# One of three shifted copies made by a pre-filled buffer and an adding DMA, in a two-kind attention stack

## The chip, the cores and the metric

The kernel runs on one core of one Trainium2 chip. The metric is device time in microseconds (us) of one execution; lower is better. The core has TensorE (PE; its weight loads are listed as PEld), VectorE (DVE), ScalarE (ACT), GpSimd (POOL), a queue that mostly issues DMAs (SP), and 16 DMA engines.

## The reference

Four residual blocks follow one another on x of 2048 rows by 512 columns, bf16: A, B, A, B with shared weights.

```python
# A: 32 query heads of 16, one shared key head and one shared value head
q = (x @ wq).reshape(B, S, H, Dh).transpose(0, 2, 1, 3); k = x @ wk; v = x @ wv
scores = einsum("bhqd,bkd->bhqk", q, k) * Dh ** -0.5
p = softmax(scores, axis=-1)
o = einsum("bhqk,bkd->bhqd", p, v)          # then heads joined, @ wo
# B: linear attention, phi(t) = where(t > 0, t + 1, exp(t)) + 1e-6
kv = einsum("bhsd,bhse->bhde", phi(k), v); z = sum over s of phi(k)
o = einsum("bhqd,bhde->bhqe", phi(q), kv) / (phi(q) . z + 1e-6)   # then @ wo
x = x + A(ln(x)); x = x + B(ln(x)); x = x + A(ln(x)); x = x + B(ln(x))
```

## The kernel before

All data stay in the core's own memory from the first load to the last store. The text calls the two A blocks layer 0 and layer 2, and the two B blocks layer 1 and layer 3. Nearly all time goes into the exponentials of A: 32 heads of 2048 by 2048 scores, cut into 4096 blocks (two layers of 2048) of 128 keys (partitions) by 512 columns, the columns being 4 heads' worth of 128 queries. Line 933 makes one block of scores in a PSUM bank, on one of four row groups of TensorE; blocks of different row groups are issued together. The blocks are grouped into segments of 64 (one query tile, one half of the heads, all 16 key tiles and 4 lanes; some segments are split by key tiles at the start of a layer). Then a block takes one of two ways:

- **The ScalarE way.** Two or three blocks at once are exponentiated by one ACTIVATE (line 1109) into a `PT` buffer, and each block is multiplied by the values with one matmul (line 987, weights `V`).
- **The VectorE way.** VectorE adds a constant to the scaled scores, clamps them and converts to int16 (line 1190). Read as bf16, these bits are a coarse power of two. To smooth it, three more copies are made with w*32 added to the bits, w = 1, 2, 3 (line 1232), and the four copies are multiplied by the values with four different weights `VW` (line 987, four matmuls). A **chunk** is up to four such blocks in one `FB` buffer of 128 x 2048 int16; the three shifted copies go to three more `FB` buffers, each with one instruction over the whole chunk.

`FB` buffers come from `fb_pool`: 12 of its own, and others that are lent while their owner is idle (`sacc` 1, `xn` 1, `wq` 1, `wo2` 1, and in layer 2 two in `OBB`). The same line of code can therefore appear in the profile as writing `FB`, `wq`, `xn`, `OBB`, `sacc` or `wo`; the page prints the buffers of `wo2` as `wo`.

Which block goes which way, and the order of instructions on each engine, is fixed when the program is built. The `Planner` runs the whole work as a simulation of events: each `op` has a duration per engine, a priority, a delay `lat` until its result is seen, and dependences; free buffers are handed out by pools; the order in which the simulation starts ops is the order written into each engine's queue, with semaphore waits. On the chip each engine then goes through its queue strictly in that order. An op that takes longer on the chip than in the plan therefore holds up whatever is queued behind the instruction that waits for it. `dve_hit` opens a chunk only while more than `FBO` buffers are free; VectorE is given a block only while its backlog is short (`dve_open`, `dve_split`, `alone`), so a faster VectorE is given more blocks. `dve_close` starts `dve_shifts`, which asks for a buffer for each shifted copy:

```python
for w in range(1, NSH):
    ...
    g_ = yield ("acq", fb_pool, pr)
    ...
    o = op({en: (du, lambda e, w=w, g_=g_: e.tensor_scalar(
        out=fbs[g_][:, 0:n].bitcast(I16), in0=fbs[f_][:, 0:n].bitcast(I16), scalar1=float(w * 128 // NSH), scalar2=None, op0=ALU.add))},
```

`spend` returns a buffer to the pool when the last of its users is done, and `pv_post` puts the blocks on the list from which `pv_try` builds groups of up to four matmuls for the segment that is being summed. Plain loads, stores and DMA transposes (`dmat`, used for 24 transposes `OT<-Osb` and 36 `xnT<-xn`) go through SP. In layers 0 and 2 POOL does one power per row tile (line 789, part of the layer norm, for which VectorE's line 792 waits) and one small product (line 836). `fill` (line 1032) gives TensorE dummy matmuls when it has nothing else to do.

Of the kernel before, what the change touches and what calls it, by code (L numbers as in the profile page):

```python
# [8 lines left out]
I16 = mybir.dt.int16  # L9
ACTF = mybir.ActivationFunctionType  # L10
ALU = mybir.AluOpType
# [4 lines left out]
P = 128  # L16
# [7 lines left out]


class Op:
    __slots__ = ("eng", "opts", "fn", "deps", "prio", "left", "users", "done", "end", "n", "value", "sem", "signal", "isdma", "name", "freed", "begun", "slot", "cols", "mode", "port")


class Pool_:  # L30
# [5 lines left out]
class Planner:  # L36
# [3 lines left out]
    def __init__(self, nc):  # L40
        self.nc = nc
        self.now = 0.0
        self.events = []
        self.seq = 0
        self.ready = {e: [] for e in ENGS}
        self.busy = {e: False for e in ENGS}
        self.until = {e: 0.0 for e in ENGS}
        self.order = {e: [] for e in ENGS}
        self.writer = {}
        self.readers = {}  # L50
        self.flags = {}
# [5 lines left out]
        self.port = 0.0  # L57
        self.calm = False
        self.hungry = []
        self.near = {e: [] for e in ENGS}  # L60
# [12 lines left out]
    def ws(self, k):  # L73
        return self.writer.get(k, [])

    def op(self, opts, reads=(), writes=(), prio=5.0, lat=0.08, dma=False, name="", join=None, mode="full", port=False, after=(), behind=()):
# [9 lines left out]
        o.port = port  # L86
        deps = set()
# [24 lines left out]
        if o.left == 0:  # L112
            self._eligible(o)
        return o
# [26 lines left out]
    def _dispatch1(self, e):  # L141
        if self.busy[e]:
            return
        h = self.ready[e]
        held = []
        while h:
            x = heapq.heappop(h)
            o = x[2]
            if o.eng is not None:
                continue  # L150
            dur, fn = o.opts[e]
            if o.port and self.port > self.now:
# [34 lines left out]
            self.at(self.now + dur + o.name[1], lambda: self._done(o))  # L187
# [105 lines left out]
    def finalize(self):  # L293
        allops = [o for e in ENGS for o in self.order[e]]
        for e in ENGS:
            for i, o in enumerate(self.order[e]):
                o.n = i
        for o in allops:
            for d in o.deps:
                if d.isdma or d.eng != o.eng or o.eng in (DV, AC, PO):  # L300
                    d.signal = True
        self.sems = {e: self.nc.alloc_semaphore("s_" + e) for e in (PE, AC, DV, PO)}
        for e in ENGS:
            c = 0
# [4 lines left out]
        dmas = [o for o in self.order[SP] if o.isdma]  # L309
        ring = [self.nc.alloc_semaphore("s_dma%d" % i) for i in range(min(RING, len(dmas)))]  # L310
        for i, o in enumerate(dmas):
            o.sem, o.value, o.slot = ring[i % RING], 16 * (i // RING + 1), i % RING
            if i >= RING:
                o.deps.add(dmas[i - RING])

    def emit(self, e, eng):
        waited = {}
# [18 lines left out]
class Seg:  # L336
# [11 lines left out]
    def take(self, js, back=False):  # L348
# [31 lines left out]
RING = 24  # L380
# [35 lines left out]
STICK = 1.5  # L416
PBL = 1.2
BACK = 2
TUNE = {0: {"FBS": 5, "AHEAD": 15, "LAG": 0.15, "ENDL": 12, "FBO": 0, "BLO": 7.0, "DXB": 1.6, "BLT": 3.2},
        2: {"FBS": 3, "DXB": 1.6, "ENDL": 9, "BLS": 1.0}}  # L420


def bass_interleave_layers__grouped_kv_mqa__linear_attn_block__prompt_kernel(
# [111 lines left out]
    def guest(L, kind, i, h=None):  # L535
        return once((L, kind, i, h), home[kind, i]) if (kind, i) in home else ()
# [119 lines left out]
    def pool_op(fn, writes, reads=(), dur=0.2, prio=0.0):  # L656
        return op({PO: (dur, fn)}, reads=reads, writes=writes, prio=prio)
# [7 lines left out]
    pool_op(lambda e: e.affine_select(identF[:], identF[:], pattern=[[-1, P]], compare_op=ALU.not_equal,  # L665
                                      fill=1.0, base=0, channel_multiplier=1), ["identF"], dur=0.3, prio=1.1)
    pool_op(lambda e: e.memset(kmask[:, 0:1], 0.0), ["kmask"], dur=0.1)
    pool_op(lambda e: e.memset(kmask[:, 1:2], KSC), ["kmask"], dur=0.1)
    for j in range(4):
        for r, v in ((0, KSC), (1, 0.0)):  # L670
# [42 lines left out]
    def until(*keys):  # L713
        for k in keys:
            yield ("ops", pl.ws(k))
# [208 lines left out]
    def run_a(L):  # L924
# [293 lines left out]
        def dve_shifts(blk, f_, hold):  # L1218
            n = 512 * len(blk)
            pr = 8.0 + 0.001 * min(x[0].i for x in blk)  # L1220
            si = min(x[0].i for x in blk)
            for w in range(1, NSH):
                while len(fb_pool.free) <= FBS and sum(x.total - x.submitted for x in segs[cur["i"]:si]) > (AHEAD if segs[si].blocks < 32 else 0):
                    yield ("sleep", 0.2)
                g_ = yield ("acq", fb_pool, pr)
# [12 lines left out]
                    o.users.append(gone)  # L1238
                spend(hold, o)
                pv_post(o, [(sg, kt, j, fbs[g_][:, h * 512:(h + 1) * 512], ("FB", g_, h)) for h, (sg, kt, j) in enumerate(blk)], [len(blk), [], fb_pool, g_], w)  # L1240

        def spare_sacc(i):
            for u in pairs[i]:
# [27 lines left out]
                lend(pt_pool, "PT", NPT + 2 + i)  # L1271

        pl.process(spare())
        for i in pairs:
            pl.process(spare_sacc(i))
        oslot = {}
# [563 lines left out]
```

## Time and profile before

| | |
|---|---|
| Time, median of 3 runs | 1510.68 us (1508.97 to 1510.83) |
| The profiled execution's own time | 1508.96 us |
| Its span | 1507.2 us |
| PE busy | 1420.5 us (94%) |
| DVE busy | 1438.6 us (95%) |
| ACT busy | 1470.6 us (98%) |
| POOL busy | 67.9 us (5%) |
| DMA bytes | 18.60 MB, mean 12 GB/s |

The profile page gives busy time by engine, the busy share in 40 slices of the span, the DMA queues, the chain of work that ended last, and the costliest groups of instructions as "line engine op out<-in xcount | busy, mean ns". Matmuls are pipelined, so a busy PE is not a PE at its peak. Views of the trace give the same for one line, one tile or one stretch of time. Times in a timeline are counted from the start of the span. The two attention stages are seen as the stretches in which line 1232 runs: about 40 to 705 us (layer 0) and 845 to 1466 us (layer 2).

### The profile page before, as it was taken

To read this page: it belongs to the slowest core of one execution; us is meant where nothing else is said; L and a number is where in the kernel's file an instruction comes from. 1 tells how busy PE (TensorE), PEld (TensorE's weight loads), DVE (VectorE), ACT (ScalarE), POOL (GpSimd) and SP (SyncE) were. 2 spreads that over 40 slices of the span, in tenths; PEclk is the share of its full clock that TensorE was granted. 3 is DMA by queue.
4 is the path that set the end of the run, shared out by engine and by line. 5 is a ranking of instruction groups with operands and counts; after the bars stand their busy time and mean duration, and the time that the engine had idled before them with its cause. 6 is when DMAs were issued, how large, how long until landed. Compare 5 with 4: busy or idle time off the path is not lost.

```text
span 1507.2 us, 35873 instructions
## 1 busy us (share of the span) xinstructions
PE 1420.5 (94%) x14512; PEld 515.1 (34%) x14630; DVE 1438.6 (95%) x2714; ACT 1470.6 (98%) x1515; POOL 67.9 (5%) x126
## 2 busy tenths in 40 slices
PE   7999999999999999999999999999999999999998
PEld 4433333222322233223744333223333333333335
DVE  7899999999999999998766899999999999999997
ACT  7999999999999999999699999999999999999996
POOL 4000000000000000000111000000000000000001
PEclk9999999999999999999999999999999999999999
DMA  4100000000000000000000000000000000000001
GB/s 110 61 8 8 9 9 5 8 5 8 8 8 8 8 5 5 2 15 16 2 2 1 2 5 16 8 9 8 8 5 8 9 8 5 8 5 1 16 2 57
DMA packets 41491, 18.60 MB, mean 12 GB/s; under 512 B 34160, under 2 KB 40816, under 8 KB 41328
## 3 DMA queue, kind: packets, MB, share of 16 engines
q1 hardware_dynamic: 41328, 16.30, 4.6%
q8 instruction: 118, 1.93, 0.6%
q14 instruction: 45, 0.37, 0.1%
HBM read 6.32 MB, written 2.10 MB: 6 GB/s over the span
## 4 chain that ended last, share of the span: by engine, by line
issue 46%; DVE 21%; PE 16%; ACT 15%; POOL 1%; DMA 0%; SPq 0%; POOLq 0%; ACTq 0%; DVEq 0%
ACT PT L1109 12%; DVE FB L1190 8%; DVE FB L1232 5%; PE ps L987 5%; PE ps L933 4%; ACT OBB L1109 3%; PE ps L705 2%; PE ps L866 2%; POOL rs L789 1%; DVE xn L1190 1%; PE ps L1032 1%; DVE sacc L1190 1%; PE ps L1309 1%; DVE sacc L1289 1%; DVE wq L1232 1%
## 5 line engine op out<-in xcount | busy, mean ns | idle before, releaser
L1109 ACT ACTIVATE PT<-ps 128x1024 bf16<-128x1024 f32 (+1 forms) x950 | 1033.5, 1203 | 3.7 <-PE ps L933 2.5
L933 PE MATMUL ps<-QT,KM 32*128 32x512 bf16 x4096 | 530.0, 385 | 39.6 <-ACT PT L1109 17.3
L987 PE MATMUL ps<-FB,VW 128*32 128x512 bf16 x3020 | 497.7, 385 | 13.5 <-ACT PT L1109 6.1
L1190 DVE TENSOR_SCALAR FB<-ps 128x512 int16<-128x512 f32 x693 | 462.1, 687 | 1.7 <-PE ps L933 0.5
L987 PE MATMUL ps<-PT,V 128*32 128x512 bf16 x2150 | 442.7, 386 | 4.5 <-ACT PT L1109 2.8
L933 PEld LDWEIGHTS ps<-QT,KM 32*128 32x128 bf16 x4096 | 132.5, 91 | 438.9 <-ACT PT L1109 217.5
L1109 ACT ACTIVATE xnT<-ps 128x1024 bf16<-128x1024 f32 (+1 forms) x238 | 266.6, 1172 | 0.5 <-PE ps L987 0.2
L1232 DVE TENSOR_SCALAR FB<-FB 128x2048 int16<-128x2048 int16 x394 | 263.5, 683 | 0.1
L1109 ACT ACTIVATE OBB<-ps 128x1024 bf16<-128x1024 f32 (+1 forms) x165 | 193.6, 1200 | 0.3
L987 PEld LDWEIGHTS ps<-FB,VW 128*32 128x32 bf16 x3020 | 122.1, 94 | 153.6 <-issue 78.9
L987 PE MATMUL ps<-xnT,V 128*32 128x512 bf16 x527 | 140.8, 385 | 0.6 <-ACT PT L1109 0.2
L1032 PE MATMUL ps<-QT,V 128*32 128x512 bf16 (+6 forms) x602 | 139.7, 315 | 0.2 <-DVE FB L1190 0.2
L987 PEld LDWEIGHTS ps<-PT,V 128*32 128x32 bf16 x2150 | 107.1, 94 | 72.5 <-issue 41.3
L987 PE MATMUL ps<-OBB,V 128*32 128x512 bf16 x374 | 108.2, 386 | 1.1 <-ACT PT L1109 0.6
L789 POOL TENSOR_TENSOR rs<-ve,mhalf 128x1 f32<-128x1 f32 x64 | 47.7, 747 | 1363.6 <-DVE ve L787 1363.4
L987 PE MATMUL ps<-xn,VW 128*32 128x512 bf16 x248 | 69.8, 384 | 2.4 <-ACT OBB L1109 1.0
L987 PE MATMUL ps<-wo,VW 128*32 128x512 bf16 x232 | 69.2, 386 | 1.1 <-ACT OBB L1109 0.5
L1032 PEld LDWEIGHTS ps<-QT,V 128*32 128x32 bf16 x602 | 47.8, 95 | 62.8 <-issue 41.9
L987 PE MATMUL ps<-wq,VW 128*32 128x512 bf16 x228 | 67.7, 386 | 1.1 <-ACT xnT L1109 0.5
L1190 DVE TENSOR_SCALAR sacc<-ps 128x512 int16<-128x512 f32 x100 | 67.3, 686 | 0.3
L705 PE MATMUL ps<-wqkv,xnT 128*128 128x512 bf16 (+1 forms) x206 | 63.5, 368 | 4.0 <-issue 2.8
L987 PE MATMUL ps<-sacc,VW 128*32 128x512 bf16 x232 | 64.2, 385 | 1.4 <-DVE sacc L1289 0.8
(191 smaller groups left out, 1600.9 us busy)
## 6 DMA issues: line engine op xcount, KB each, us to landing
out_dram<-x_sb SPq DMA_DIRECT2D x16, 128.0 KB, 1.7
x_sb<-in_A_x_dram SPq DMA_DIRECT2D x3, 512.0 KB, 6.6
wqkv<-in_B_wqkv_dram SPq DMA_DIRECT2D x1, 1536.0 KB, 7.5
wq<-in_A_wq_dram SPq DMA_DIRECT2D x2, 512.0 KB, 4.1
wo<-in_B_wo_dram SPq DMA_DIRECT2D x2, 512.0 KB, 4.0
xnT<-xn SPq DMA_TRANSPOSE x36, 2.5
x_sb<-in_A_x_dram SPq DMA_DIRECT2D x4, 128.0 KB, 2.2
wo<-in_A_wo_dram SPq DMA_DIRECT2D x1, 512.0 KB, 4.1
```

The lines of the kernel that those rows point to most:

```text
L705: return e.matmul(dst, lhsT=l, rhs=r, start=(k == 0), stop=(k == len(pairs) - 1))
L789: op({PO: (0.55, lambda e: e.tensor_tensor(out=rs[:, t:t + 1], in0=ve[:, t:t + 1], in1=mhalf[:], op=ALU.pow))}, reads=[("ve", t), "mhalf"] ...
L866: ins = e.matmul(dst[:, g * P:(g + 1) * P], lhsT=lhs(g, k), rhs=rhs(k), start=(k == 0), stop=(k == FT - 1))
L933: return e.matmul(bank(b), lhsT=KM[r, sg.par, kt * P:(kt + 1) * P], rhs=QT[r, sg.t, :], start=True, stop=True)
L987: ins = e.matmul(ps[32 * j:32 * j + 32, ACC * 512:(ACC + 1) * 512], lhsT=V[:, kt, :] if w is None else VW[:, kt, w, :], rhs=ap, start=(k = ...
L1032: o = op({PE: (n / 2400.0, lambda e: e.matmul(ps[32 * j:32 * j + 32, b * 512:b * 512 + n], lhsT=V0[:], rhs=QT[:, sg.t, 0:n], start=st, sto ...
L1109: ex = op({AC: (0.051 + 0.4267 * n, lambda e, n=n, s_=s_, p_=p_: e.activation(pts[p_][:, 0:n * 512], ps[:, s_ * 512:(s_ + n) * 512], ACTF. ...
L1190: o = op({DV: (0.602, lambda e: e.tensor_scalar(out=dst.bitcast(I16), in0=bank(b), scalar1=VB, scalar2=VLO, op0=ALU.add, op1=ALU.max))}, w ...
L1232: o = op({en: (du, lambda e, w=w, g_=g_: e.tensor_scalar(out=fbs[g_][:, 0:n].bitcast(I16), in0=fbs[f_][:, 0:n].bitcast(I16), scalar1=float ...
L1289: o = op({DV: (0.6, lambda e, src=src: e.tensor_copy(src, bank(ACC)))}, writes=[B_(ACC), key], prio=0.0, lat=0.15, behind=host(L, key) if ...
L1309: o = op({PE: (0.12, lambda e, c=c: e.transpose(ps[:, b * 512 + c * P:b * 512 + (c + 1) * P], src[:, c * P:(c + 1) * P], identF[:]))}, rea ...
```

## The change

When a full chunk of four blocks is closed, the copy with w = 1 (`DSH`) may be made without VectorE. A process `prime`, one in each A layer, takes a free `FB` buffer, if more than `FBP` = 6 are free and nobody waits, and lets SP fill it with the constant 32 by a DMA that reads one 4 KB row of DRAM for all 128 partitions; at most `NPRE` = 2 such buffers stand ready or are being filled. `dve_shifts` takes one of them for a full chunk, unless the chunk is in the last `DMIN` = 4 segments or the planner's account of the DMA engines (`dmaq`) is more than `DQ` = 4 us behind. Then POOL issues a DMA that adds the chunk's buffer (512 KB) into the filled one. Otherwise the copy is made on VectorE as before. The planner books the fill as 0.54 us of SP, 0.2 us, 2.5 us of the DMA engines and 2.5 us until it is seen; the add as 1.1 us of POOL, 0.3 us, 4.5 us of the DMA engines and 2.5 us. At the start POOL writes the row once and SP stores it to DRAM. DMAs issued by POOL get a ring of `PRING` = 8 semaphores of their own.

```diff
+            end = self.now + dur + o.name[1]
+            if o.xfer:
+                self.dmaq = max(end, self.dmaq) + o.xfer[0]
+                end = self.dmaq + o.xfer[1]
+            self.at(end, lambda: self._done(o))
...
+        for q, n in ((SP, RING), (PO, PRING)):
+            dmas = [o for o in self.order[q] if o.isdma]
...
+PRING = 8
+DSH = 1
+DMIN = 4
+NPRE = 2
+PGEN = 1.1
+DPF = 2.5
+DXF = 4.5
+DTAIL = 2.5
+DQ = 4.0
+FBP = 6
...
+    cst = nc.dram_tensor("shift_row", (1, CHB * 512), I16, kind="Internal").ap()
...
+    pool_op(lambda e: e.memset(FB[:, NFB - 1, :].bitcast(I16), DSH * 128 // NSH), fb_keys(NFB - 1), dur=1.2, prio=8.0)
+    op({SP: (0.54, lambda e: e.dma_start(cst, FB[0:1, NFB - 1, :].bitcast(I16)))}, reads=fb_keys(NFB - 1), writes=["cst"], prio=8.0, lat=2.5, dma=True)
...
-            for w in range(1, NSH):
+            ws = list(range(1, NSH))
...
+            if len(blk) == CHB and primed and si < len(segs) - DMIN and pl.dmaq < pl.now + DQ:
+                ws.remove(DSH)
+                dma_shift(blk, f_, hold, *primed.pop(0))
+            for w in ws:
...
+        def prime():
+            yield ("flag", ("K", L, T - 1))
+            yield from until("cst")
+            while state["si"] < len(segs) - DMIN:
+                if len(primed) >= NPRE or len(fb_pool.free) <= FBP or fb_pool.wait:
+                    yield ("sleep", 0.2)
+                    continue
+                g_ = yield ("acq", fb_pool, 9.0)
+                o = op({SP: (0.54, lambda e, g_=g_: e.dma_start(fbs[g_].bitcast(I16), cst.to_broadcast([P, CHB * 512])))}, reads=["cst"], writes=fb_keys(g_), prio=9.0,
+                       lat=0.2, dma=True, behind=guest(L, "FB", g_), xfer=(DPF, DTAIL))
+                primed.append((g_, o))
...
+        def dma_shift(blk, f_, hold, g_, o):
...
+            o = op({PO: (PGEN, lambda e: e.dma_start(fbs[g_].bitcast(I16), fbs[f_].bitcast(I16), accum_op=ALU.add))}, reads=fb_keys(f_), writes=fb_keys(g_), prio=0.0, lat=0.3,
+                   dma=True, xfer=(DXF, DTAIL))
+            spend(hold, o)
+            pv_post(o, [(sg, kt, j, fbs[g_][:, h * 512:(h + 1) * 512], ("FB", g_, h)) for h, (sg, kt, j) in enumerate(blk)], [len(blk), [], fb_pool, g_], DSH)
```

More of the change, by code (lines that the diff above doesn't have):

```diff
@@ L26 @@
 class Op:
-    __slots__ = ("eng", "opts", "fn", "deps", "prio", "left", "users", "done", "end", "n", "value", "sem", "signal", "isdma", "name", "freed", "begun", "slot", "cols", "mode", "port")
+    __slots__ = ("eng", "opts", "fn", "deps", "prio", "left", "users", "done", "end", "n", "value", "sem", "signal", "isdma", "name", "freed", "begun", "slot", "cols", "mode", "port", "xfer")
 class Pool_:
@@ L57, in __init__ @@
         self.port = 0.0
+        self.dmaq = 0.0
+        self.stat = {"dma": 0, "chunk": 0, "blk": 0}
         self.calm = False
@@ L74, in ws, with op @@
         return self.writer.get(k, [])
-    def op(self, opts, reads=(), writes=(), prio=5.0, lat=0.08, dma=False, name="", join=None, mode="full", port=False, after=(), behind=()):
+    def op(self, opts, reads=(), writes=(), prio=5.0, lat=0.08, dma=False, name="", join=None, mode="full", port=False, after=(), behind=(), xfer=None):
         o = Op()
@@ L86, in op @@
         o.port = port
+        o.xfer = xfer
         deps = set()
@@ L186, in _dispatch1 @@
             self.at(self.now + dur, lambda: self._freed(e, o))
-            self.at(self.now + dur + o.name[1], lambda: self._done(o))
+            end = self.now + dur + o.name[1]
[3 more added lines that the diff above has]
+            self.at(end, lambda: self._done(o))
             break
@@ L308, in finalize @@
                     o.sem, o.value = self.sems[e], c
[L309 to L314, printed above, removed]
+        for q, n in ((SP, RING), (PO, PRING)):
+            dmas = [o for o in self.order[q] if o.isdma]
+            ring = [self.nc.alloc_semaphore("s_dma_%s%d" % (q, i)) for i in range(min(n, len(dmas)))]
+            for i, o in enumerate(dmas):
+                o.sem, o.value, o.slot = ring[i % n], 16 * (i // n + 1), (q, i % n)
+                if i >= n:
+                    o.deps.add(dmas[i - n])
     def emit(self, e, eng):
@@ L667, in bass_interleave_layers__grouped_kv_mqa__linear_attn_block__prompt_kernel, with fb_keys @@
     pool_op(lambda e: e.memset(kmask[:, 0:1], 0.0), ["kmask"], dur=0.1)
+    cst = nc.dram_tensor("shift_row", (1, CHB * 512), I16, kind="Internal").ap()
+    def fb_keys(i):
+        return [("FB", i, h) for h in range(CHB)]
+    pool_op(lambda e: e.memset(FB[:, NFB - 1, :].bitcast(I16), DSH * 128 // NSH), fb_keys(NFB - 1), dur=1.2, prio=8.0)
+    op({SP: (0.54, lambda e: e.dma_start(cst, FB[0:1, NFB - 1, :].bitcast(I16)))}, reads=fb_keys(NFB - 1), writes=["cst"], prio=8.0, lat=2.5, dma=True)
     pool_op(lambda e: e.memset(kmask[:, 1:2], KSC), ["kmask"], dur=0.1)
@@ L1221, in dve_shifts @@
             si = min(x[0].i for x in blk)
-            for w in range(1, NSH):
+            ws = list(range(1, NSH))
+            pl.stat["chunk"] += 1
+            pl.stat["blk"] += len(blk)
+            if len(blk) == CHB and primed and si < len(segs) - DMIN and pl.dmaq < pl.now + DQ:
+                ws.remove(DSH)
+                dma_shift(blk, f_, hold, *primed.pop(0))
+            for w in ws:
                 while len(fb_pool.free) <= FBS and sum(x.total - x.submitted for x in segs[cur["i"]:si]) > (AHEAD if segs[si].blocks < 32 else 0):
@@ L1240, in dve_shifts @@
                 pv_post(o, [(sg, kt, j, fbs[g_][:, h * 512:(h + 1) * 512], ("FB", g_, h)) for h, (sg, kt, j) in enumerate(blk)], [len(blk), [], fb_pool, g_], w)
+        primed = []
+        def prime():
[9 more added lines that the diff above has]
+                primed.append((g_, o))
+            while primed:
+                g_, o = primed.pop()
+                pl.give_after(fb_pool, g_, [o])
+        def dma_shift(blk, f_, hold, g_, o):
+            pl.stat["dma"] += 1
+            o = op({PO: (PGEN, lambda e: e.dma_start(fbs[g_].bitcast(I16), fbs[f_].bitcast(I16), accum_op=ALU.add))}, reads=fb_keys(f_), writes=fb_keys(g_), prio=0.0, lat=0.3,
+                   dma=True, xfer=(DXF, DTAIL))
+            spend(hold, o)
+            pv_post(o, [(sg, kt, j, fbs[g_][:, h * 512:(h + 1) * 512], ("FB", g_, h)) for h, (sg, kt, j) in enumerate(blk)], [len(blk), [], fb_pool, g_], DSH)
         def spare_sacc(i):
@@ L1273, in run_a @@
         pl.process(spare())
+        pl.process(prime())
         for i in pairs:
```

## The prediction

> **What bounds the kernel now.** I read the busy table first, then the busy time by stretches for the two attention stages, then the same stretches for the lines that make and consume the exponentials. The columns of a stretch are its ends, its length, the busy us of the engines with their instruction counts, the granted clock, the DMA engines' busy share and GB/s.
>
> ```profile
> PE 1420.5 (94%) x14512; PEld 515.1 (34%) x14630; DVE 1438.6 (95%) x2714; ACT 1470.6 (98%) x1515; POOL 67.9 (5%) x126
> ```
>
> ```profile
> 40.00:705.00 665.00, 627.68 (x6385) 207.69 (x6436) 660.71 (x1190) 663.87 (x657) 14.64 (x18) 1.00 0.05 11
> 845.00:1466.00 621.00, 592.07 (x6044) 199.49 (x6094) 619.22 (x1122) 619.00 (x633) 15.52 (x15) 1.00 0.04 7
> ```
>
> In both attention stages ACT and DVE are busy for all but 1 to 4 us of 665 and 621. Neither waits for the other: two full workers share 4096 blocks, and the split decides when both end. PE reads 94% too, but its busy time is modelled from overlapping instructions; what it really has left is seen below, in its dummy matmuls.
>
> The same stretches for single lines: the VectorE shifts (L1232),
>
> ```profile
> 40.00:705.00 665.00, 268.00 (x403) 1.00 0.05 11
> 845.00:1466.00 621.00, 250.19 (x374) 1.00 0.04 7
> ```
>
> the VectorE evictions (L1190),
>
> ```profile
> 40.00:705.00 665.00, 361.19 (x543) 1.00 0.05 11
> 845.00:1466.00 621.00, 332.04 (x499) 1.00 0.04 7
> ```
>
> the ScalarE exponentials (L1109),
>
> ```profile
> 40.00:705.00 665.00, 656.33 (x631) 1.00 0.05 11
> 845.00:1466.00 621.00, 608.99 (x601) 1.00 0.04 7
> ```
>
> and the score matmuls (L933) and value matmuls (L987), PE before PEld:
>
> ```profile
> 40.00:705.00 665.00, 247.81 (x1972) 62.27 (x1969) 1.00 0.05 11
> 845.00:1466.00 621.00, 234.86 (x1820) 58.71 (x1820) 1.00 0.04 7
> ```
>
> ```profile
> 40.00:705.00 665.00, 328.17 (x3562) 83.42 (x3565) 1.00 0.05 11
> 845.00:1466.00 621.00, 292.77 (x3300) 72.89 (x3304) 1.00 0.04 7
> ```
>
> There are 1042 blocks on VectorE (543 + 499) and 777 shifts (403 + 374), so nearly every chunk is full: 777 / 3 = 259 chunks, one per 1286 / 259 = 5.0 us. ScalarE takes 3792 - 1042 = 2750 blocks in 1265.3 us, 0.46 us each.
>
> ```profile
> 399.89 1.28 DVE L1190 TENSOR_SCALAR FB<-ps 128x512 int16<-128x512 f32 x2
> ...
> 403.68 1.29 DVE L1232 TENSOR_SCALAR FB<-FB 128x2048 int16<-128x2048 int16 x2
> 404.88 0.69 DVE L1190 TENSOR_SCALAR FB<-ps 128x512 int16<-128x512 f32 x1
> ```
>
> In the timeline the two shifts begin at 403.68 and the next instruction at 404.88, so one shift takes 0.60 us of VectorE's queue although its own duration is 0.69; an eviction the same (two span 1.28, 0.69 of it the last). One VectorE block thus costs 0.60 + 3/4 x 0.60 = 1.05 us, against 0.46 on ScalarE.
>
> **What one moved copy is worth.** It takes 0.60 us off VectorE. The planner hands VectorE more blocks when its backlog falls, so both workers end earlier. If d blocks change sides per moved copy, VectorE saves 0.60 - 1.05 d and ScalarE 0.46 d; equal at d = 0.40, which is 0.183 us of the stage per moved copy, not 0.60. The d blocks cost PE three more value matmuls each. L987 is busy 620.9 us for 6862 matmuls, 0.09 us each, so 0.40 x 3 x 0.09 = 0.11 us per moved copy. What hides this are the dummies, which PE runs only when nothing else is ready:
>
> ```profile
> 40.00:705.00 665.00, 68.03 (x298) 23.34 (x298) 1.00 0.05 11
> 845.00:1466.00 621.00, 64.27 (x281) 22.57 (x281) 1.00 0.04 7
> ```
>
> These 132 us of L1032 cover 110 x 0.11 = 12 us. Without that cover the 12 us would be paid.
>
> **How many copies move.** The plan books 2.5 + 4.5 = 7.0 us of the DMA engines per moved copy and refuses one when more than 4 us behind, so at most 1286 / 7.0 = 184. The other gate is a spare buffer: a fill is started only while more than six are free. Here is the life of two single buffers, `wq` in layer 0 and `xn` in layer 2; the rows are a shift that writes it and the first and last matmuls that read it.
>
> ```profile
> 417.94 0.68 DVE L1232 TENSOR_SCALAR wq<-FB 128x2048 int16<-128x2048 int16 x1
> 422.81 0.39 PE L987 MATMUL ps<-wq,VW 128*32 128x512 bf16 x2
> 424.12 0.38 PE L987 MATMUL ps<-wq,VW 128*32 128x512 bf16 x1
> 439.03 0.68 DVE L1232 TENSOR_SCALAR wq<-FB 128x2048 int16<-128x2048 int16 x1
> 443.03 0.59 PE L987 MATMUL ps<-wq,VW 128*32 128x512 bf16 x4
> ...
> 1106.88 0.66 DVE L1232 TENSOR_SCALAR xn<-wo 128x2048 int16<-128x2048 int16 x1
> 1107.96 0.39 PE L987 MATMUL ps<-xn,VW 128*32 128x512 bf16 x1
> 1126.79 0.69 DVE L1232 TENSOR_SCALAR xn<-FB 128x2048 int16<-128x2048 int16 x1
> 1128.52 0.38 PE L987 MATMUL ps<-xn,VW 128*32 128x512 bf16 x1
> ```
>
> `wq` holds data from 417.94 to 424.50 and nothing until 439.03: 14.5 of 21.1 us. Part of this is free time, part the wait of a promised buffer for VectorE. Of the 16 buffers of layer 0 about 11 hold no data, but some of these are promised; six is thus a gate that opens often and not always. The change itself takes buffers out of it: a filled one waits for its chunk, and the source chunk stays until the add has landed. I estimate 110 moved copies of 259; the bounds are 0 and 184. That gives -110 x 0.183 = -20 us, between 0 and -34.
>
> **The add and the fill, which no row shows.** In the trace every transfer is issued by SP, and none adds. The nearest rows:
>
> ```profile
> wqkv<-in_B_wqkv_dram SPq DMA_DIRECT2D x1, 1536.0 KB, 7.5
> ...
> wo<-in_B_wo_dram SPq DMA_DIRECT2D x2, 512.0 KB, 4.0
> xnT<-xn SPq DMA_TRANSPOSE x36, 2.5
> ```
>
> 512 KB land in 4.0 us and 1536 KB in 7.5, so 512 KB more cost 1.75 us. The fill moves 512 KB: 4.0 us, against 5.74 booked; it is a copy of one row 128 times, and I allow up to 7.5. The add reads two buffers and writes one: 4.0 us if a second read is free, 7.5 if it counts like two more passes. I take 5.75, one extra pass. Before it POOL has to prepare it: 0 at the least, 1.1 us as booked, and up to 1.0 more from the rows below. So 4.0 to 9.6 us, taken 7.2; the plan books 1.1 + 0.3 + 4.5 + 2.5 = 8.4. At my value the data are there before PE's queue asks, and the cost is nothing; that cover is 1.2 us thin, and the upper end is 1.2 us past it.
>
> Behind a wait that comes too late stands all of PE's queue: the value matmul that reads the added copy waits, the next scores are behind it, and ACT runs dry after the set it holds. How soon PE reads a copy is in the rows of the two buffers: the shifts end at 418.62, 439.71, 1107.54 and 1127.48 and are first read 4.2, 3.3, 0.4 and 1.0 us later. About half leave under 1 us.
>
> POOL now issues 110 DMAs between its layer-norm powers, of which VectorE's L792 waits:
>
> ```profile
> 305.16 0.68 DVE L1232 TENSOR_SCALAR FB<-FB 128x2048 int16<-128x2048 int16 x1
> 305.32 0.93 POOL L789 TENSOR_TENSOR rs<-ve,mhalf 128x1 f32<-128x1 f32 x1 [34.05 <-DVE ve L787]
> ```
>
> ```profile
> 439.72 0.69 DVE L1289 COPY sacc<-ps 128x512 f32<-128x512 f32 x1
> 439.85 0.55 POOL L789 TENSOR_TENSOR rs<-ve,mhalf 128x1 f32<-128x1 f32 x1 [48.11 <-DVE ve L787]
> ```
>
> ```profile
> L789 POOL TENSOR_TENSOR rs<-ve,mhalf x64: 543/550/1530, 4.2 to 1475.4; 128x1 f32<-128x1 f32 x64
> ```
>
> The power takes 0.55 us beside a copy out of PSUM but 0.93 where it began 0.16 us into a shift; of all 64 (shortest, median, longest in ns) the worst takes 1.53, 1.0 more. So a shift keeps POOL waiting, and the add's preparation, which begins just when the chunk's other shifts become ready, will be held up likewise. That is the 1.0 above. The plan does not know of it. The Trainium skill, "SBUF — State Buffer", section "A bandwidth-pool intuition that's wrong (but worth ruling out)", says that a DMA issued by POOL took about 620 ns alone and 3100 ns beside a VectorE copy, because its descriptors could not be written meanwhile. By that, as an estimate from the page, an add would land 2.5 us later than without shifts, about 1 us past the plan's booking; the rows above agree that POOL is held, but show at most 1.0 us.
>
> In a POOL queue of 33 instructions in both stages (x18 and x15 above) an add in front of a power costs up to 1.1 us, which the plan has placed; 0 to 2 us in all, taken 1. The transposes (24 of `OT`, and those of `xnT`, mostly in these stages) share the DMA engines with 220 new transfers: 2.5 us to landing, 1.75 more behind a fill makes 4.25, against 4.1 booked (0.1 issue and `DTL` 4.0). Only one caught behind two transfers is late by more than a little, about 1.9 us: some ten at most, 0 to 20 us, taken 3. The set-up (one POOL memset of 1.2 us and a 4 KB store) lies in the first 40 us, at the lowest priority: 0 to 1.2 us, taken 0.
>
> **The sum.** -20 + 1 + 3 = -16 on the profiled execution's 1508.96 us: 1493. The median of the runs shown is 1.7 us above that execution, so 1494.7, say 1494.
>
> **The rivals.**
>
> R1, the add lands later than booked: slower. For it: the upper bound of 9.6 us, and a fill that may be slow and hold up the add. Against it: 7.2 us in my sum. Each lateness counts only beyond the slack of 0.4 to 4.2 us. If it is 2 us late, the four rows above would lose 1.6, 1.0, 0 and 0, mean 0.65 us; 110 x 0.65 = 72 us if ACT gets nothing from the ready set, half of it if that set covers half. Taken three quarters, 54: 1494 + 54 = 1548. At 1.1 us late they lose 0.7, 0.1, 0 and 0, which by the same three quarters is 110 x 0.20 x 0.75 = 16 us, all of the gain; from there on it is slower.
>
> R2, POOL takes the memory path first and VectorE's shifts wait: slower. The rows show POOL held by a shift; the reverse would hold VectorE for the 1.1 us of preparation at each add, since two shifts follow at once. Then a moved copy loses 1.1 - 0.60 = 0.5 us of VectorE instead of saving 0.60: 110 x 0.5 x 0.183 / 0.60 = +17, and +4 from the sum: 1531. It decides from 0.60 us per add on. Against it: no shift in the trace is longer beside POOL's powers (0.68 against 0.69), but these touch one element per partition. The Trainium skill, "SBUF — State Buffer", section "Who interferes with whom", has this rule: whichever of the two starts first keeps the shared ports for its whole instruction. No run here shows it for a DMA of POOL.
>
> R3, little moves: the buffers are seldom spare, some 20 copies go, -4 and a re-shuffled plan of about +-4: 1507. For it: the change takes buffers from the pool that it asks. Against it: `wq` empty for 14.5 of 21.1 us.
>
> **How the numbers follow.** About 0.2%, 3 us, is what a measurement of this kernel can tell from no change. The forecast gets 0.50 (0.48 faster, 0.02 the same), R1 0.27 (0.25 slower, 0.01 each of the others), R2 0.13 (0.10 slower, 0.02 the same, 0.01 faster), R3 0.10 (0.05 faster, 0.03 the same, 0.02 slower): faster 0.55, same 0.08, slower 0.37. The range begins at 1478, where 184 copies move at no cost (1508.96 - 34 + 1.7 = 1477), and reaches to 1545, which holds R2, R3 and the milder half of R1. The forecast's own range is 1478 to 1506.
>
> **What would show it.** Right: about 110 DMAs issued by POOL; in the two stretches about 1085 evictions (1042 + 110 x 0.40) and about 700 shifts (3 x 1085 / 4 - 110) in place of 777; ACT and DVE are still full in both stages, and those DMAs land within about 8 us. R1: adds landing beyond 8.4 us, and waits of PE for a DMA of tens of us, with ACT below 98% of the stages. R2: shifts at the adds well above 0.69 us, or DVE idle that ends with POOL. R3: fewer than 40 DMAs from POOL. The prediction is wrong if ACT or DVE shows gaps in the stages, or if the time leaves 1478 to 1545.

## The result and the profile after

The changed kernel takes 1502.70 us (median of 5 runs, 1501.63 to 1505.49) against 1510.68 for the kernel before (5 runs, 1507.02 to 1515.43): 8.0 us less, a ratio of 0.9951 with a 95% interval of 0.9927 to 0.9974. That is faster by 0.5%, clear of the noise since the interval lies below 1, and it is inside the range, but it is a little under half of the 16.7 us that were forecast. So the mechanism has to be looked for.

The page of the profile after, its busy line; then the busy time of the two attention stages (span of the stretch, then PE, PEld, DVE, ACT, POOL, the granted clock, the DMA share, GB/s), and the same stretches for the evictions (L1215, before L1190) and the shifts (L1263, before L1232):

```profile
span 1501.0 us, 36621 instructions
...
PE 1418.2 (94%) x14634; PEld 514.3 (34%) x14745; DVE 1426.3 (95%) x2684; ACT 1453.6 (97%) x1519; POOL 167.2 (11%) x230
```

```profile
40.00:705.00 665.00, 631.13 (x6502) 209.68 (x6544) 659.34 (x1187) 660.77 (x666) 59.58 (x64) 1.00 0.36 86
845.00:1460.00 615.00, 586.99 (x6015) 192.49 (x6055) 608.32 (x1101) 610.46 (x630) 67.55 (x72) 1.00 0.45 104
```

```profile
40.00:705.00 665.00, 371.78 (x566) 1.00 0.36 86
845.00:1460.00 615.00, 342.63 (x519) 1.00 0.45 104
```

```profile
40.00:705.00 665.00, 247.61 (x375) 1.00 0.36 86
845.00:1460.00 615.00, 222.70 (x333) 1.00 0.45 104
```

Evictions rise from 1042 to 1085, the number that the prediction named, and shifts fall from 777 to 708 (named: 700). So the work has changed sides as worked out. ACT's work falls too: 1470.6 us busy before, 1453.6 after, 17.0 less. But the span falls by 6.2 only (1507.2 to 1501.0), because ACT is idle for 1501.0 - 1453.6 = 47.4 us where it was idle for 36.6. The missing time is idle time of ACT, 10.8 us of it. About half of it lies in the two attention stages, where ACT's gaps grow from 1.1 to 4.2 us and from 2.0 to 4.5; the other 5 us are spread over the start, layer 1 and the end. What ended the gaps in front of the exponentials is in the view of their line, first before (L1109), then after (L1134):

```profile
its engine sat idle before it (us, times) until:
  PE ps L933: 2.5, 5
  PE ps L987: 0.7, 3
```

```profile
its engine sat idle before it (us, times) until:
  PE ps L1012: 5.2, 8
  PE ps L958: 3.3, 8
  PE ps L891: 1.1, 1
```

L933 and L958 are the score matmuls, L987 and L1012 the value matmuls. All these gaps end with a matmul of PE, 3.2 us of them before and 9.6 after, and what grows most are those that end with a value matmul.

The new transfers, from the page and from the view of the adds' line (1292) with the time from issue to landing:

```profile
FB<-shift_row SPq DMA_DIRECT2D x81, 512.0 KB, 4.6
FB<-FB POOLq DMA_DIRECT2D x56, 512.0 KB, 5.0
```

```profile
L1292 POOL DMA_DIRECT2D FB<-FB x56: 852/872/1367, 50.6 to 1357.4; - x56
...
who waited for it (us, times):
busy tenths in 40 slices 0100001000000100000000000001111010100000
DMA to landing us min/median/max: 4.5/5.0/10.7
```

An add lands 5.0 us after its issue at the median, under the 8.4 that are booked; the latest takes 10.7. The list of those who waited for an add is empty, so the changed kernel does not lose its time by waiting for adds. The line's rows over all buffers sum to 103 adds; the prediction had 110.

### The profile page after: what moved, and what is told of

Read it like the earlier page. It is cut to its first block, busy times and chain, and to the rows that moved or that the text cites. A ratio compares the mean times of both kernels' runs of the same rounds, so it can differ in the third digit from the quotient of the medians.

```text
span 1501.0 us, 36621 instructions
## 1 busy us (share of the span) xinstructions
PE 1418.2 (94%) x14634; PEld 514.3 (34%) x14745; DVE 1426.3 (95%) x2684; ACT 1453.6 (97%) x1519; POOL 167.2 (11%) x230
## 4 chain that ended last, share of the span: by engine, by line
PE 35%; DVE 33%; ACT 24%; issue 7%; POOL 0%; ACTq 0%; POOLq 0%
ACT PT L1134 16%; PE ps L1012 13%; DVE FB L1215 12%; PE ps L958 11%; DVE FB L1263 8%; PE ps L730 4%; ACT xnT L1134 3%; ACT OBB L1134 3%; PE ps L891 2%; DVE OBB L1215 2%; PE ps L1057 2%; PE ps L1365 1%; DVE sacc L1215 1%; DVE xn L1215 1%; DVE wq L1263 1%
## 5 line engine op out<-in xcount | busy, mean ns | idle before, releaser
L1134 ACT ACTIVATE PT<-ps 128x1024 bf16<-128x1024 f32 (+1 forms) x951 | 1016.4, 1179 | 6.3 <-PE ps L1012 3.0
L958 PE MATMUL ps<-QT,KM 32*128 32x512 bf16 x4096 | 536.5, 385 | 43.0 <-ACT PT L1134 18.0
L1215 DVE TENSOR_SCALAR FB<-ps 128x512 int16<-128x512 f32 x790 | 521.0, 682 | 5.6 <-PE ps L958 4.4
L1012 PE MATMUL ps<-FB,VW 128*32 128x512 bf16 x3126 | 501.5, 385 | 9.5 <-ACT PT L1134 3.1
L1012 PE MATMUL ps<-PT,V 128*32 128x512 bf16 x2108 | 431.4, 386 | 2.2 <-ACT PT L1134 1.3
L958 PEld LDWEIGHTS ps<-QT,KM 32*128 32x128 bf16 x4096 | 134.1, 91 | 442.2 <-ACT PT L1134 216.2
L1134 ACT ACTIVATE xnT<-ps 128x1024 bf16<-128x1024 f32 (+1 forms) x241 | 267.8, 1158 | 3.7 <-PE ps L1012 2.0
L1263 DVE TENSOR_SCALAR FB<-FB 128x2048 int16<-128x2048 int16 (+1 forms) x354 | 237.2, 678 | 0.3
L1134 ACT ACTIVATE OBB<-ps 128x1024 bf16<-128x1024 f32 (+1 forms) x167 | 190.1, 1170 | 1.2 <-PE ps L958 0.5
L1012 PEld LDWEIGHTS ps<-FB,VW 128*32 128x32 bf16 x3126 | 123.3, 94 | 146.9 <-issue 86.0
L1012 PE MATMUL ps<-xnT,V 128*32 128x512 bf16 x530 | 144.5, 385 | 0.7 <-ACT xnT L1134 0.3
L1057 PE MATMUL ps<-QT,V 128*32 128x512 bf16 (+6 forms) x571 | 132.1, 316 | 0.8 <-DVE FB L1215 0.4
L1012 PEld LDWEIGHTS ps<-PT,V 128*32 128x32 bf16 x2108 | 104.8, 94 | 70.5 <-issue 44.4
L1012 PE MATMUL ps<-OBB,V 128*32 128x512 bf16 x372 | 108.9, 385 | 1.5 <-ACT PT L1134 0.5
L1292 POOL DMA_DIRECT2D FB<-FB x56 | 52.1, 930 | 422.0 <-DVE FB L1215 247.6
L1012 PE MATMUL ps<-xn,VW 128*32 128x512 bf16 x256 | 69.3, 384 | 0.1
L1012 PE MATMUL ps<-sacc,VW 128*32 128x512 bf16 x246 | 68.2, 384 | 0.7 <-ACT PT L1134 0.6
L1012 PE MATMUL ps<-wq,VW 128*32 128x512 bf16 x244 | 64.2, 384 | 1.2 <-ACT PT L1134 1.1
L1012 PE MATMUL ps<-OBB,VW 128*32 128x512 bf16 x240 | 58.5, 385 | 3.2 <-ACT PT L1134 1.4
```

The lines of the kernel that those rows point to most:

```text
L958: return e.matmul(bank(b), lhsT=KM[r, sg.par, kt * P:(kt + 1) * P], rhs=QT[r, sg.t, :], start=True, stop=True)
L1012: ins = e.matmul(ps[32 * j:32 * j + 32, ACC * 512:(ACC + 1) * 512], lhsT=V[:, kt, :] if w is None else VW[:, kt, w, :], rhs=ap, start=(k = ...
L1057: o = op({PE: (n / 2400.0, lambda e: e.matmul(ps[32 * j:32 * j + 32, b * 512:b * 512 + n], lhsT=V0[:], rhs=QT[:, sg.t, 0:n], start=st, sto ...
L1134: ex = op({AC: (0.051 + 0.4267 * n, lambda e, n=n, s_=s_, p_=p_: e.activation(pts[p_][:, 0:n * 512], ps[:, s_ * 512:(s_ + n) * 512], ACTF. ...
L1215: o = op({DV: (0.602, lambda e: e.tensor_scalar(out=dst.bitcast(I16), in0=bank(b), scalar1=VB, scalar2=VLO, op0=ALU.add, op1=ALU.max))}, w ...
L1263: o = op({en: (du, lambda e, w=w, g_=g_: e.tensor_scalar(out=fbs[g_][:, 0:n].bitcast(I16), in0=fbs[f_][:, 0:n].bitcast(I16), scalar1=float ...
```

## The experiments

Each kernel ran in five rounds against the kernel before on the same chip, whose median there was 1508.3 to 1509.2 us.

**Copies left out, with nothing in their place.** The chunk's own buffer is read in place of the copy w = 1.

```diff
+            ws = list(range(1, NSH))
+            pl.nchunk = getattr(pl, "nchunk", 0) + 1
+            if len(blk) == CHB and pl.nchunk % 5 < 2:      # skip_all: every full chunk
+                ws.remove(1)
+                hold[0] += len(blk) - 1
+                pv_post(pl.ws(("FB", f_, CHB - 1))[-1], [(sg, kt, j, fbs[f_][:, h * 512:(h + 1) * 512], ("FB", f_, h)) for h, (sg, kt, j) in enumerate(blk)], hold, 1)
+            for w in ws:
```

> The kernel before, in which no full chunk gets its copy w = 1: the matmuls with the weights of w = 1 read the unshifted chunk instead. So VectorE loses 0.60 us of work for each of about 262 copies, and no DMA, no fill and no extra buffer takes their place. Theory A (the sum of the prediction is right, 0.183 us of the end for each copy taken off VectorE, and in the changed kernel the adding DMAs lose the rest): 262 x 0.183 = 48 us less than before, about 1463. Theory B (a copy taken off VectorE is worth clearly less than 0.183 even where nothing is paid for it): about 0.12 to 0.15 each, 1471 to 1479. Theory C (it is worth only what the changed kernel gained, 0.07 each): about 1492.

Measured: 1473.28 us, 35 less. Its page:

```profile
PE 1402.8 (95%) x14697; PEld 500.0 (34%) x14809; DVE 1401.9 (95%) x2647; ACT 1422.9 (97%) x1538; POOL 67.3 (5%) x126
```

The faster VectorE takes 1177 blocks in place of 1045, so there are 1177 / 4 = 294 chunks and not 262: 0.12 us for each copy left out. ACT's work falls by 47.7 us, 0.16 for each, near the 0.18 of the sum; its idle time grows by 11.7 (span 1471.2). That is the time of theory B, and no DMA is needed for it. ScalarE's work falls by less than 132 blocks at 0.46 us would give (61 us). A part of that is that it takes more of its blocks two at a time: 180 of its exponentials do three blocks, where 345 did before, and in the timeline of before a step over two takes 0.91 us and one over three 1.33.

> As the kernel without the copies w = 1, but only two of five chunks lose theirs, about 105 copies, as many as the changed kernel moved to DMAs (103). What is left out is that copy; the matmuls of w = 1 read the unshifted chunk there. Theory A (0.183 each, the loss is in the DMA way): 19 us less than before, about 1492. Theory B (less than 0.183 for each): 13 to 16 us less, 1495 to 1498. Theory C (nothing is lost in the DMA way): the same time as the changed kernel, 1503.

Measured: 1498.97, 9.4 less for 110 copies, between theories B and C: 0.09 each. The same picture: ACT busy 1452.8, 17.8 less, but idle 44.2 instead of 36.6.

**The same work in another order.** One booked delay of the planner is shifted by 0.1, 0.3 or 0.5 ns; nothing else.

```diff
-EX_LAT = 0.185
+EX_LAT = 0.1851      # or 0.1853, 0.1855
```

> The kernel before with one booked delay of the planner changed from 0.1850 to 0.1851 us: the same work in another order. Theory D (the order is a draw, before's a lucky one): 1508 to 1522. Theory E (order does not matter): within 3 us of 1510.7.

> The kernel before with one booked delay of the planner changed from 0.1850 to 0.1853 us. The same work is done, in another order on the engines. Theory D (before's order is one draw of many, and a lucky one; every change draws again): 1508 to 1520, above before on the mean of several such kernels. Theory E (order of this kind does not matter): within 3 us of 1510.7.

> The kernel before with the booked delay at 0.1855 us: the same work in a third order. Theory D: 1508 to 1522. Theory E: within 3 us of 1510.7.

> The changed kernel with the booked delay at 0.1851 us. Theory D: 1495 to 1515, and less than the kernel before at 0.1851 by 5 to 14 us on the mean of the three pairs. Theory E: within 3 us of 1502.7.

> The changed kernel with the same booked delay changed from 0.1850 to 0.1853 us. Theory D (the order is a draw): another time than 1502.7 by up to 10 us either way, with the difference to the equally shifted kernel before larger than the 8 us seen, since before's luck is gone. Theory E: within 3 us of 1502.7.

> The changed kernel with the booked delay at 0.1855 us. Theory D: 1495 to 1515. Theory E: within 3 us of 1502.7.

> Two of five chunks without the copy w = 1 (the matmuls of w = 1 read the unshifted chunk), with the booked delay at 0.1851 us. Beside before at this delay (1521.15) and the changed kernel (1517.77). Sum of the prediction: 1502. Worth of 0.12 to 0.15: 1505 to 1508. If the DMA way loses nothing: 1517.

> Two of five chunks without the copy w = 1 (the matmuls of w = 1 read the unshifted chunk), with the booked delay at 0.1853 us. Beside the other kernels at this delay (before 1512.5, changed 1507.2) it gives what 105 copies are worth when nothing takes their place. Sum of the prediction: 19 us below before's 1512.5, 1493. A lower worth of 0.12 to 0.15: 1496 to 1500. If the DMA way loses nothing: 1507.

> The same with the booked delay at 0.1855 us. Beside before at this delay (1518.35) and the changed kernel (1506.49). Sum of the prediction: 1499. Worth of 0.12 to 0.15: 1502 to 1506. If the DMA way loses nothing: 1506. Since each order is a draw, only the mean of the three such kernels against the means of the others counts.

Measured, in us (medians):

| booked delay | before | changed | two of five copies left out |
|---|---|---|---|
| 0.1850 | 1510.68 | 1502.70 | 1498.97 |
| 0.1851 | 1521.15 | 1517.77 | 1506.08 |
| 0.1853 | 1512.51 | 1507.16 | 1504.87 |
| 0.1855 | 1518.35 | 1506.49 | 1496.42 |
| mean | 1515.7 | 1508.5 | 1501.6 |

Theory D holds: nearly the same work (1045 to 1055 blocks on VectorE in the kernels before) in another order takes up to 10 us more, and the orders of the two kernels as given are better than their neighbours, before's by 2 to 10 us and the changed kernel's by 4 to 15. So the draw is not what halved the gain: on the mean of four orders the change is worth 7.1 us (3.4 to 11.9), about what was seen. My further expectation, that the difference would grow without before's luck, fell. Copies that cost nothing are worth 14.1 us (7.6 to 21.9), 0.13 each. The DMA way loses 6.9 us against them (2.3 to 11.7). Taken as ratios to the kernel before on the same chip, the three means are 6.9, 14.1 and 7.2 us. The four differences of the free copies scatter so widely that the 20 us of the prediction's sum (110 x 0.183) are not excluded by them alone.

The busy lines of before and of the changed kernel at 0.1853:

```profile
PE 1424.6 (94%) x14573; PEld 517.8 (34%) x14688; DVE 1444.5 (96%) x2722; ACT 1468.4 (97%) x1506; POOL 69.0 (5%) x126
```

```profile
PE 1423.9 (95%) x14671; PEld 515.9 (34%) x14781; DVE 1430.5 (95%) x2695; ACT 1453.5 (97%) x1521; POOL 166.8 (11%) x229
```

ACT's work hardly depends on the order: 1468.4 to 1472.9 us in the four kernels before, 1453.5 to 1454.6 in the four changed ones. What the order moves is ACT's idle time: 36.6 us in before, 42.5 to 46.5 at the other delays; 47.4 after, 50.7 to 64.1 at the others. On the mean of the four orders ACT works 1470.8 us before, 1453.8 in the changed kernels and 1453.3 in those without the copies, and is idle for 42.2, 53.5 and 48.4 us. So the change takes 17.0 us of work from ACT and gives 11.3 us of idle time back, more at every delay (by 7.3 to 17.6). Of these 11.3 us 8.3 stand in front of its exponentials (5.9 us there before, 14.2 changed, 9.3 without the copies), and most of that rise is in gaps that end with a value matmul (1.6 us before, 8.5 changed, 3.3 without the copies).

**PE relieved.** The value matmuls of w = 2 and 3 are left out, with and without the copies w = 1.

```diff
+                    if w in (2, 3):
+                        spend(hold, src)
+                        continue
                     sg.ready.append((kt, j, ap, key, hold, w))
...
-                hit[0].need[hit[2]] += NSH - 1
-                hit[0].total += NSH - 1
+                hit[0].need[hit[2]] += NSH - 1 - 2
+                hit[0].total += NSH - 1 - 2
```

> The kernel before without the value matmuls of the copies w = 2 and w = 3; VectorE still makes these copies. This takes about 2090 of 8190 L987 matmuls from PE and nothing from VectorE or ScalarE. It is the reference for the next kernel. If PE's dummies cover its work, as the prediction has it, the time stays within 5 us of before; if PE is part of the bound, it falls by more.

> The kernel without the copies w = 1 (matmuls of w = 1 read the unshifted chunk) and, as its reference, without the value matmuls of w = 2 and 3. Theory H (the copy is worth less than 0.183 because the blocks that change sides load PE with three more matmuls each): with PE relieved each of about 270 copies is worth more than in the kernel that only lacks the copies, 0.16 to 0.18 us, 43 to 48 us less than its reference. Theory I (PE has no part in it): the same worth as there.

Measured: 1512.92 and 1462.63, 50.3 us for 290 copies (1160 blocks on VectorE), 0.17 each, where the copies alone gave 0.12. That speaks for theory H: with PE relieved, a copy is worth nearly what the sum said, and the matmuls would be part of what makes ACT wait. ACT's work falls by 48.3 us, as without relief (47.7); what is smaller is the growth of its idle time, 3.7 us against 11.7, and no gap in front of an exponential ends with a value matmul any more. But this is one order of each kernel, and 50.3 against 35 is a difference of 15 us where an order alone moves a time by 10, so it is a sign and not a proof. Relief by itself gains nothing (1512.92), which was to be the sign that PE is no part of the bound before the change.

**Shorter bookings, more copies.**

```diff
-DPF = 2.5
-DXF = 4.5
-DTAIL = 2.5
+DPF = 2.0
+DXF = 3.0
+DTAIL = 2.0
```

> The changed kernel with shorter bookings: fill 2.0 instead of 2.5 us of the DMA engines, add 3.0 instead of 4.5, and 2.0 instead of 2.5 us until either is seen. An add is then booked to be seen 6.4 us after POOL takes it, where the trace of the changed kernel has 5.0 us (median, longest 10.7) from its issue to its landing. Buffers come back 2 us sooner and the gate of 4 us opens more often. Theory F (part of the gain is lost because the bookings hold buffers longer than the transfers need): more than 103 copies move, 5 to 8 us faster than the changed kernel, 1495 to 1498. Theory G (the bookings are needed; adds that land late stop PE): slower than the changed kernel, with PE waits for a DMA of tens of us.

Measured: 1521.96 us, 19 slower than the changed kernel. The view of the adds in this kernel:

```profile
who waited for it (us, times):
  PEld ps L1012: 13.8, 8
  PE ps L1012: 11.0, 8
busy tenths in 40 slices 0001001010010010000000000111111111110000
DMA to landing us min/median/max: 4.5/5.1/10.4
```

Now eight adds come after PE needs them, although the median landing is as before: it is the late ones that count. The same with two gates opened further (`FBP` 4, `DMIN` 1) and the delay at 0.1846:

> The kernel with shorter bookings, with the gate for a fill at four free buffers instead of six, allowed up to the last segment but one instead of four, and the booked delay at 0.1846 us. Theory F: about 200 copies move; at 0.12 each 24 us below the typical order of before, so 1486 to 1493, faster than every kernel so far that does all the work. Theory G: late adds eat this; 1500 or more.

Measured: 1532.69 us. One of its late adds in the timeline (start, us, engine, line, tiles, and in brackets the idle time before and what ended it):

```profile
179.84 0.39 PE L1012 MATMUL ps<-PT,V 128*32 128x512 bf16 x2
...
184.15 0.61 PE L1012 MATMUL ps<-PT,V 128*32 128x512 bf16 x1 [3.92 <-DMA FB<-FB]
...
185.36 1.02 ACT L1134 ACTIVATE PT<-ps 128x1024 bf16<-128x1024 f32 x1 [3.91 <-PE ps L958]
185.36 0.69 DVE L1215 TENSOR_SCALAR FB<-ps 128x512 int16<-128x512 f32 x1 [3.62 <-PE ps L958]
```

and the stretch in which it lies:

```profile
180.00:190.00 10.00, 6.08 (x35) 1.37 (x32) 4.48 (x8) 4.52 (x5) 0.76 (x1) 0.66 0.79 170
```

PE waits 3.92 us for an add, and ACT and VectorE wait 3.9 and 3.6 us behind it: ready data cover next to nothing of this wait. Then PE's matmuls take 0.61 us instead of 0.39; the granted clock of these 10 us is 0.66. A late add is paid twice. The Trainium skill, "TensorE: Matmul & The Clock Gate", section "Part 1: The HAM clock gate (the "warmup" mystery)", has the clock go to half after an idle window of about 3.4 us; the 3.92 us here agree. Shorter waits were enough, though, in the kernel with shorter bookings alone (1521.96 us). Its longest wait for an add, with PE's busy time, the granted clock, the DMA share and GB/s in 2 us stretches:

```profile
1245.91 0.61 PE L1012 MATMUL ps<-PT,V 128*32 128x512 bf16 x1 [2.93 <-DMA wo<-FB]
```

```profile
1242.00:1244.00 2.00, 0.98 (x16) 1.00 1.01 221
1244.00:1246.00 2.00, 0.09 (x4) 0.70 0.75 266
1246.00:1248.00 2.00, 2.00 (x19) 0.50 0.01 4
```

The clock stays at 0.50 until about 1258, 12 us; behind another wait, of 2.26 us, it falls to 0.50 for about 7 us. Over this whole execution the granted clock is 0.992.

**The transfers cut short, in the same order.** Every instruction, wait and buffer stays; adds and fills (but the first fill of each buffer in a layer) move 64 of 4096 bytes of a row.

```diff
-... e.dma_start(fbs[g_].bitcast(I16), cst.to_broadcast([P, CHB * 512])))}
+... e.dma_start(fbs[g_].bitcast(I16)[:, 0:m_], cst[:, 0:m_].to_broadcast([P, m_])))}      # m_ = 32, or whole the first time
-... e.dma_start(fbs[g_].bitcast(I16), fbs[f_].bitcast(I16), accum_op=ALU.add))}
+... e.dma_start(fbs[g_].bitcast(I16)[:, 0:32], fbs[f_].bitcast(I16)[:, 0:32], accum_op=ALU.add))}
```

> The changed kernel in its very order, with the transfers cut to 64 bytes of each row of 4096: every add, and every fill but the first of each buffer in a layer. What is left out is the rest of the filled and added copy. Every instruction, every wait and every buffer is where it was. Theory J (the missing gain is lost on the chip while 103 MB cross the DMA engines: late adds, slower neighbours): about 1492 to 1495. Theory K (nothing is lost there, the missing gain is in the order and in the buffers that wait): within 3 us of 1502.7.

> The kernel with shorter bookings (1521.96) in its very order, with the transfers cut to 64 bytes of each row in the same way. Theory G (that kernel is slow because adds land after PE needs them, and nothing else): 15 us or more faster than 1521.96, 1493 to 1502. The rival (its order is a bad draw): within 5 us of 1521.96.

Measured: 1500.97 and 1498.48 us. The changed kernel gains 1.7 us without most of its bytes, at the edge of what the runs tell, and nothing when each time is set against before on its own chip (ratios 0.9951 and 0.9952). That is theory K: its loss is not in the bytes that it moves. POOL's issues, 0.87 us each, and the waits stay in this kernel and are not tested by it. The kernel with shorter bookings gains 23.5 us: its order is good, and lateness alone made it slow. An estimate of the two payments: PE waited 11.0 us for adds, and a clock of 0.992 where this kernel without the bytes has 1.000 is 12 us of 1518, together about the 21 us between the two profiled spans (1517.6 and 1496.5).

**More copies at the old bookings.**

```diff
-FBP = 6
+FBP = 4
-EX_LAT = 0.185
+EX_LAT = 0.1853
```

> The changed kernel with its bookings kept, the gate for a fill at four free buffers instead of six, and the booked delay at 0.1853 us. About 130 copies move instead of 103. If adds that are booked as in the changed kernel still land in time at this density, 1490 to 1500, faster than both kernels; if the DMA engines fall behind the bookings, PE waits for adds, 1500 or more.

Measured: 1497.35 us for 134 copies, the least of the kernels with all transfers; one add was waited for, for 0.6 us. Its output is wrong, for a cause that I did not find, so this is a time of its order and no version to use. No kernel here that does all the work is a better version than the changed one.

## Why the prediction was right or wrong

**The copies and the sides: right.** 103 copies moved (110 forecast; that it came so close is in part luck, since the 110 was picked between bounds of 0 and 184), 41 blocks changed sides (1045 to 1086 over the whole run, 0.40 for each copy), and ACT's work fell by 17.0 us (0.46 x 41 = 18.9). The difference is in how the blocks are grouped: 59 more exponentials of two blocks, at 0.91 us, and 53 fewer of three, at 1.33, make 16.8.

**"One moved copy is worth 0.183 us": this step failed.** It set the end equal to the work of two full workers. The work moved as worked out, but ACT did not stay full, which the prediction had named as a sign that it is wrong: its idle time ate 10.8 of 17.0 us, and 11.3 of 17.0 on the mean of four orders. The copy moved by DMA came to 0.07 to 0.08 us. That much is shown. That a copy is worth less than 0.183 even where it costs nothing is likely and not shown: 0.12 us each in the one kernel without them, 0.14 if its time is set against the mean of before's four orders, and 0.13 on the mean of the four with two of five left out, each within the scatter of an order. Why ACT waits more is shown only in part. That before has a tight order (36.6 us of idle, others 42.5 to 46.5) and that a new order starts from scratch, for which I had allowed 4 us in R3 alone, is true of these two traces, but over four orders of each the gain is no larger, so the draw of the order is not the cause. PE is the likelier one: I let its dummies cover 12 us of matmuls, but they still run for 124.6 us in the stages (132.3 before) while ACT's gaps, which end with PE's matmuls, have grown; and with PE relieved a copy came to 0.17. That a dummy is there does not mean that the matmul which ACT waits for could have run in its place. On one order of each, the cause stays open.

**The cost of the DMA way: mis-sized.** I priced it at 4 us for neighbours on POOL and on the DMA engines. The neighbours cost next to nothing: VectorE waits for POOL's powers 7 times, 3.1 us in all (7 times and 3.9 before), and of the 60 transposes one was waited for, 0.7 us. The difference to free copies is 6.9 us on the mean of four orders, and the kernel without the bytes, on one order, puts about 1.7 of it or nothing in the transfers. The rest would then be in the plan, where 4.9 us more stand in front of ACT's exponentials than in the kernels with free copies. What the trace shows there is how long a buffer is taken, from the issue of its fill to the issue of its add. Two of 17 such pairs, fill and add in the same single buffer (`wo`, `wq` or `xn`), from the timelines of SP and POOL:

```profile
987.03 0.32 SPq L1283 DMA_DIRECT2D wo<-shift_row  x1
...
1317.01 0.78 SPq L1283 DMA_DIRECT2D wq<-shift_row  x1
```

```profile
1002.20 0.86 POOL L1292 DMA_DIRECT2D wo<-FB  x1 [10.92 <-DVE FB L1215]
...
1322.14 0.86 POOL L1292 DMA_DIRECT2D wq<-OBB  x1 [7.55 <-DMA FB<-shift_row]
```

15.2 and 5.1 us; the mean of the 17 is 12.8, of which the fill itself takes 4.6 at the median, and in the second pair POOL waited for a fill. With 5.0 until the add lands, a moved copy holds its buffer for 18 us before anyone can read it, where a shift needs 0.6. 103 x 18 / 1286 is 1.4 buffers gone at all times, besides the source that waits. That these buffers cost the 5 us, or the value matmuls that wait for a copy and hold up ACT's `PT` buffers, was not tried apart from the rest and stays open.

**R1: the mechanism is real, its condition was not met.** Adds land in 5.0 us, less than the 7.2 in my sum, and none was waited for. At shorter bookings it costs 23.5 us, which is the rival; my "ready set" that would cover part of a wait covered nearly nothing of the one shown, and the fall of the clock was missing in its price.

**R2: no.** Shifts last 683 ns at the median (687 before), 781 at the most (716 before); POOL's adds are issued in 0.87, and the longest took 2.83. It lies beside five shifts in a row, of which the first two and the last are shown, and ends 0.12 us after the last of them:

```profile
249.00 1.29 DVE L1263 TENSOR_SCALAR FB<-wo 128x2048 int16<-128x2048 int16 x2
...
251.41 0.69 DVE L1263 TENSOR_SCALAR FB<-FB 128x2048 int16<-128x2048 int16 x1
```

```profile
249.39 2.83 POOL L1292 DMA_DIRECT2D FB<-xn  x1 [6.48 <-DVE xn L1215]
```

So shifts hold POOL now and then, here for 2.0 us where I had allowed 1.0, and POOL does not hold VectorE. The Trainium skill's case in "SBUF — State Buffer", section "A bandwidth-pool intuition that's wrong (but worth ruling out)", 2.5 us more (an estimate from its two figures) for a transfer beside VectorE's copies, was not met as a rule: adds cut to 64 bytes a row land in 2.1 us at the median beside the same shifts, whole ones in 5.0; only the late ones, up to 10.7, could be such.

**R3: no.** 103 copies moved.

## What to carry to other kernels

Where several engines are full, price the work that is moved and the idle time that the new order brings as two terms, and read them apart: busy time of the bounding engine, and span minus busy time. Where a planner writes the order, a shift of 0.1 ns in a booking moved the time by 10 to 15 us here, so judge a change over several orders of both kernels, not by one of each. A transfer that another engine waits for in a fixed order has to be booked by its late cases and not by its median, and a wait on TensorE costs its clock as well.

## What was not expected of the hardware

An adding DMA of 512 KB between two buffers lands in 5.0 us (4.5 to 10.7), 1.0 us more than a plain load of the same size from DRAM (4.0), while POOL is taken for 0.87 us. Copying one 4 KB row of DRAM to 128 partitions takes 4.6 us. And a single wait of 3.9 us on PE stretched its matmuls from 0.39 to 0.61 us afterwards; waits of 2.26 and 2.93 us also brought the granted clock down to 0.50, for about 7 and 12 us.
